# Weight pairs' high and low parts in new homes, the third pair made in the first FFN pass, rows of sums issued every second product

## The chip, the cores and the metric

The kernel runs on one core of one Trainium2 chip. The metric is the device time of one execution in microseconds, lower is better. TensorE (PE) multiplies, VectorE (DVE) and ScalarE (ACT) do the arithmetic around it, GpSimd (POOL) helps in the first half, and SyncE (SP) issues nearly all transfers (DMAs).

## The reference

Attention in which a query sees only the keys of its own hash bucket, and then a feed-forward layer (FFN) over all 3072 tokens. Inputs and output are float32.

```python
q, k, v: (4, 8, 768, 64); proj: (64, 6); w_in: (512, 2048); w_out: (2048, 512)
bucket = sum(2**n * (x @ proj > 0)[n])            # for q and for k
scores = where(q_bucket == k_bucket, q @ k.T / 8, -1e9)
attn   = exp(scores - max);  attn = attn / (attn.sum() + 1e-9)
x      = (attn @ v) of the heads side by side      # (3072, 512)
h      = x @ w_in
g      = h if h >= 1, 0 if h <= -1, (h + 1)**2 / 4 between
out    = g @ w_out
```

## The kernel before

Float32 accuracy comes from splitting each operand into a high part, rounded to the type float32r, and the rest, the low part: a product is then three matmuls, high x high, low x high, high x low.

The first half, to about 470 us, is attention, head after head. It leaves x unnormalised in DRAM, along with the sums to divide by, and prepares most weights on the way. This text is about the second half, `ffn`, which has two stages.

In the **first pass** the two chunks of 384 tokens of batch 0 go through the FFN in 32 steps (`gemm1`, L795 to L805, one f tile of 128 hidden features a step; N1 = 32). In the **second stage** the three other batches are computed with seven products in place of eight (a Strassen-Winograd scheme over two token chunks and two f tiles): L882 to L932 run 168 products, 7 for each of 8 pairs of f tiles for each of 3 batches. Here product k is number k from the first pass's end; the code writes it N1 + k. A product is six matmuls of 384 columns (L898), and between products four to six matmuls of 512 columns of the second layer are issued from a queue (`issue`, L674). The seven results combine in two PSUM banks and three SBUF tiles: after product s of a pair VectorE or ScalarE reads the bank (L902 to L918; s = 1 is L905), and products 2, 3 and 6 add onto a bank that was read before.

The seven products need seven blocks of weights for each pair, kept in DRAM (`wc`): blocks 0 to 2 are copies (`w_plain`), blocks 3 to 6 are sums and differences, made on the chip once, while the first batch's products already run. A pair's four sums are made so: `w_get` (the fetch, L740, L741) brings raw weights into `tmp`; `w_sum` in three parts makes the four sums in `sum_w` on VectorE (its subtractions have line 39, that of the helper `sub`); `w_hi` rounds them on ScalarE into `hi_w`, the other half of `tmp`; `w_lo` subtracts in place, so that the low parts replace the sums in `sum_w`; `w_put` (the put, L756, L757) sends both parts, 512 KB each, to `wc`. `w_plan` says in which step each of this happens. `sum_w` has one buffer: the next pair's first sum can only start when the put of the low parts has landed. Before, pairs 0 and 1 are made in the first pass, pair 2 by product 5, and pair i from there at 7 (i - 2): its fetch is in product 7 (i - 2) - 3, its sums in + 1 and + 2, its put in + 5.

The products' weights come back through a ring of nine slots (`w_load`, L775, 256 KB each), each issued eight products ahead.

The x operands of a batch (`x_plan`) need x in pieces (`x_raw`, L691, into `pcs`), rows of sums spread over the partitions (`x_er`, two transfers of 192 KB a step, L537, into a place that `spread` names and that is not in use yet, the home of an operand that is made later), normalisation on VectorE (`x_norm`, L698 and L700), sums (L709), high and low parts. Two sets of homes (`sets`: pieces of `big`, `ta`, `tb`, `tu`, `tmp`, all tiles of earlier use) serve the batches in turn.

The order of the instructions on each engine is written out by hand: `at` puts a function ahead of a step's or product's matmuls, `after` behind them, and each engine works through its own list in order, held up by the semaphores of what it needs. SyncE too is one list: a transfer that has to wait holds up all behind it.

Of the kernel before, what the change touches and what calls it, by code (L numbers as in the profile page):

```python
# [11 lines left out]
F32 = mybir.dt.float32  # L12
# [562 lines left out]
def ffn(ctx, tc, wpair, woh, wol, xm, xa, xb, areas, wst, wq, wc, out, prep, post, staged):  # L575
# [35 lines left out]
    def spread(b, cc, k):  # L611

        if b > 1:
            x = sets[(b - 1) % 2]
            n = (14, 16, 18, 25)[k]
            t, n = (tb, 6) if x is sets[1] and n == 14 else (big, n + 12) if x is sets[1] and n < 20 else (
                tu, 0) if x is sets[1] else (big, n)
        else:
            t, n = (ta, 2 * k) if cc == 1 else (tflat, 2 * k) if k < 2 else (sflat, 0) if k == 2 else (
                pcs.rearrange("p k n -> p (k n)"), 4)  # L620
        return t[:, n * CH:(n + 2) * CH].bitcast(F32).rearrange("p (t n) -> p t n", t=2)
# [126 lines left out]
    def w_hi(n):  # L748
        nc.scalar.copy(out=hi_w[:, 2 * n:2 * n + 2], in_=sum_w[:, 2 * n:2 * n + 2])

    def w_lo(n):
        sl = slice(2 * n, 2 * n + 2)
        sub(nc, nc.vector, sum_w[:, sl].bitcast(F32R), sum_w[:, sl], hi_w[:, sl].bitcast(F32))

    def w_put(i):
        nc.sync.dma_start(out=wc[i][:, 3:7, 0], in_=hi_w.bitcast(F32))  # L756
        nc.sync.dma_start(out=wc[i][:, 3:7, 1], in_=sum_w)  # L757

    def w_plan(i, get, first, second, his, los, put):
        at(get, w_get, i)  # L760
        at(first, w_sum, 0)
        at(second, w_sum, 1)
        at(second, w_sum, 2)
        for t in range(2):
            after(his[t], w_hi, t)
            at(los[t], w_lo, t)
        at(put, w_put, i)
# [48 lines left out]
    w_plan(0, 21, 24, 25, (25, 25), (26, 26), 27)  # L816
    w_plan(1, 26, 28, 29, (29, 29), (30, 30), 31)
    w_plan(2, 30, N1 + 1, N1 + 2, (N1 + 2, N1 + 3), (N1 + 4, N1 + 4), N1 + 5)
    for i in range(3, NFT // 2):
        n = N1 + NBLK * (i - 2)  # L820
        w_plan(i, n - 3, n + 1, n + 2, (n + 2, n + 3), (n + 4, n + 4), n + 5)
    x_plan(1, 0, 8, (8, 9, 10, 11), (11, 12, 13, 14), range(15, 22))
    x_plan(1, 1, 22, (24, 24, 25, 25), (26, 26, 27, 27), (28, 28, 29, 29, 30, 30, 31))
    x_plan(2, 0, N1 + 6, range(N1 + 6, N1 + 10), [N1 + n for n in (13, 14, 17, 20)],
           [N1 + n for n in (21, 24, 27, 28, 31, 34, 35)])
    x_plan(2, 1, N1 + 37, [N1 + n for n in (28, 30, 32, 34)], [N1 + n for n in (41, 42, 44, 46)],
# [10 lines left out]
    at(30, ring_staged)  # L837
# [290 lines left out]
```

## Time and profile before

| | us |
|---|---|
| median of 3 runs | 1004.57 (1003.85, 1004.57, 1008.62) |
| profiled execution | 1005.65, its span 1003.9 |
| busy in the span: PE, DVE, ACT, POOL | 972.9, 794.0, 680.7, 344.3 |
| first product of the second stage starts | 600.87 |

Times in the rows are microseconds from the start of the span. A timeline row has the start, the duration, the engine, the line and the operation, what it writes and reads (buffer numbers are left out: `t` stands for several tiles, among them a slot of the ring), and in brackets how long the engine was idle before it and what ended that. A row with x6 is six instructions merged. Line 898 is a product's matmuls. The number of a product can be counted from 600.87; one takes about 2.2 us, so product 10 starts at 622.77. Durations of matmuls overlap, so the steps between their starts count. Engines that wait for a transfer wait for its landing, of which a row of the chain of waits gives the time: a row that begins with DMA runs from issue to landing.

### The profile page before, as it was taken

What the parts mean: (1) busy time and instruction counts of PE and PEld (TensorE: products, weight loads), DVE (VectorE), ACT (ScalarE), POOL (GpSimd) and SP (SyncE); (2) the same over time, 40 slices, a digit from 0 to 9 for tenths busy, and PEclk for the clock granted to TensorE, in tenths of its full rate; (3) what the DMA queues carried; (4) which work ended last, traced back from release to release, by engine and by line L of the source; (5) the groups of instructions that cost most, each with busy time, mean ns of one, the idle gap of its engine ahead of it and who ended that gap; (6) DMA issues with size and microseconds to landing.
All of it is one profiled execution on the core that took longest, in us unless ns stands there. A gap on an engine that the chain in (4) does not pass through costs nothing.

```text
span 1003.9 us, 15529 instructions
## 1 busy us (share of the span) xinstructions
PE 972.9 (97%) x5036; PEld 891.9 (89%) x5036; DVE 794.0 (79%) x1356; ACT 680.7 (68%) x1489; POOL 344.3 (34%) x412
## 2 busy tenths in 40 slices
PE   5899999999999999999999999799999999999997
PEld 4789999999999999999999998688888898888896
DVE  7678999999999999886998687678766677655553
ACT  5778889988999888888655465355554455554443
POOL 6666778778877777656000000000000000000000
PEclk9999999999999999999999999899999999999999
DMA  2646667666666666645494358878549564454431
GB/s 90 164 113 150 174 186 196 188 179 161 173 161 171 175 174 184 156 111 131 141 329 138 116 196 262 253 225 262 149 141 247 146 185 117 134 163 116 117 84 64
DMA packets 94170, 166.19 MB, mean 166 GB/s; under 512 B 13833, under 2 KB 51337, under 8 KB 94089
## 3 DMA queue, kind: packets, MB, share of 16 engines
q1 hardware_dynamic: 93872, 165.19, 58.5%
q8 instruction: 40, 0.66, 0.3%
q14 instruction: 42, 0.34, 0.1%
q10 hardware_dynamic: 216, 0.00, 0.0%
HBM read 106.13 MB, written 33.87 MB: 139 GB/s over the span
## 4 chain that ended last, share of the span: by engine, by line
PE 84%; DVE 6%; ACT 4%; DMA 3%; issue 1%; SPq 0%; POOL 0%; ACTq 0%; DVEq 0%
PE y L674 23%; PE h L898 15%; PE smax L258 7%; PE h L802 7%; PE o L332 6%; PE s L298 6%; PE o L330 6%; PE o L331 6%; PE s L297 6%; DMA t<-ed 2%; PE o L178 2%; DVE nm L262 2%; DMA wc<-sumw 1%; ACT t L633 1%; DVE nm L359 1%
## 5 line engine op out<-in xcount | busy, mean ns | idle before, releaser
L306 ACT ACTIVATE ph<-s 128x384 fp32r<-128x384 f32 x380 | 188.4, 496 | 45.1 <-PE s L298 38.0
L262 DVE TENSOR_REDUCE nm<-smax 128x1 f32<-128x768 f32 x186 | 176.2, 947 | 16.3 <-PE smax L258 14.5
L39 POOL TENSOR_TENSOR pl<-pf,ph 128x384 fp32r<-128x384 f32 x128 | 141.7, 1112 | 79.1 <-ACT pf L311 78.6
L639 DVE SCALAR_TENSOR_TENSOR t<-t 128x384 f32<-128x384 f32 x128 | 71.3, 557 | 115.4 <-ACT z L634 115.2
L39 DVE TENSOR_TENSOR pl<-s,ph 128x384 fp32r<-128x384 f32 x256 | 135.7, 545 | 14.8 <-ACT s L311 14.1
L297 PE MATMUL s<-t 128*128 128x384 f32 x384 | 132.0, 344 | 0.8 <-DVE t L212 0.8
L332 PE MATMUL o<-pl,va 128*128 128x386 f32 x384 | 130.3, 339 | 0.3 <-DVE pl L39 0.3
L330 PE MATMUL o<-ph,va 128*128 128x386 f32 x384 | 130.2, 339 | 0.0
L298 PE MATMUL s<-t 128*128 128x384 f32 x384 | 130.1, 339 | 0.0
L331 PE MATMUL o<-ph,vb 128*128 128x386 f32 x384 | 129.4, 337 | 0.0
L311 ACT ACTIVATE s<-s 128x384 f32<-128x384 f32 x252 | 125.5, 498 | 0.0
L674 PE MATMUL y<-t,ghi 128*128 128x512 f32 x384 | 125.5, 398 | 0.0
L258 PE MATMUL smax<-t 128*128 128x384 f32 x372 | 101.5, 353 | 5.6 <-DVE nm L262 4.5
L898 PE MATMUL h<-wbig,t 128*128 128x384 f32 x399 | 83.0, 341 | 5.4 <-DVE wsq L905 5.4
L644 ACT CAST ghi<-z 128x384 fp32r<-128x384 f32 x129 | 65.1, 505 | 29.1 <-DVE z L640 25.8
L633 ACT ACTIVATE t<-h,mh 128x384 f32<-128x384 f32 x56 | 32.5, 581 | 77.1 <-PE h L802 48.3
L258 PEld LDWEIGHTS smax<-t 128*128 128x128 f32 x372 | 63.7, 188 | 22.5 <-DVE nm L262 21.3
L898 PEld LDWEIGHTS h<-wbig,t 128*128 128x128 f32 x399 | 71.9, 190 | 12.6 <-DVE wsq L905 6.7
L633 ACT ACTIVATE t<-wsq,mh 128x384 f32<-128x384 f32 x48 | 29.6, 617 | 77.5 <-DVE wsq L911 44.6
L674 PEld LDWEIGHTS y<-t,ghi 128*128 128x128 f32 x384 | 71.9, 189 | 11.2 <-ACT ghi L644 0.3
L634 ACT ACTIVATE z<-t,m 128x384 f32<-128x384 f32 x128 | 79.0, 617 | 4.2
L674 PE MATMUL y<-woh,ghi 128*128 128x512 f32 x192 | 75.6, 394 | 0.7 <-ACT ghi L644 0.7
(153 smaller groups left out, 2143.8 us busy)
## 6 DMA issues: line engine op xcount, KB each, us to landing
t<-wc SPq DMA_DIRECT2D x92, 256.0 KB
t<-t SPq DMA_DIRECT2D x60, 384.0 KB
wraw<-wc SPq DMA_DIRECT2D x76, 256.0 KB
raw<-in_qk_dram SPq DMA_DIRECT2D x15, 768.0 KB
wraw<-in_w_in_dram SPq DMA_DIRECT2D x16, 512.0 KB
wraw<-in_w_out_dram SPq DMA_DIRECT2D x16, 512.0 KB
xd<-xs SPq DMA_DIRECT2D x32, 192.5 KB
vraw<-in_v_dram SPq DMA_DIRECT2D x16, 384.0 KB
```

The lines of the kernel that those rows point to most:

```text
L39: eng.tensor_tensor(out=out, in0=a, in1=b, op=ALU.subtract)
L258: nc.tensor.matmul(out=smax[hd][:, hf, 0:HS], lhsT=t2[:, 0, h, i * P:(i + 1) * P], rhs=t2[:, 1, h, hf * HS:(hf + 1) * HS], start=True, sto ...
L262: nc.vector.tensor_reduce(out=nmp(hd)[:, i:i + 1], in_=smax[hd][:, :, 0:HS], axis=AX.XY, op=ALU.max, negate=True)
L297: nc.tensor.matmul(out=ps[:, 0:HS], lhsT=t1[:, 1, h, ks], rhs=t1[:, 0, h, sl], start=True, stop=False)
L298: nc.tensor.matmul(out=ps[:, 0:HS], lhsT=t2[:, 1, h, ks], rhs=t2[:, 0, h, sl], start=False, stop=True)
L306: nc.scalar.activation(out=ph[:, 0:HS], in_=ps[:, 0:HS], func=AF.Exp, scale=SCALE)
L311: nc.scalar.activation(out=pf, in_=ps[:, 0:HS], func=AF.Exp, scale=SCALE)
L330: nc.tensor.matmul(out=o, lhsT=wa, rhs=ph, start=(jj == 0), stop=False)
L331: nc.tensor.matmul(out=o, lhsT=wb, rhs=ph, start=False, stop=False)
L332: nc.tensor.matmul(out=o, lhsT=wa, rhs=pl, start=False, stop=(jj == NJ - 1))
L674: nc.tensor.matmul(out=ys[c][m], lhsT=g_[:, m * P:(m + 1) * P], rhs=w, start=(first and k == 0), stop=(last and k == 2))
L898: nc.tensor.matmul(out=ps, lhsT=w[:, cs], rhs=x, start=(n == 0 and s not in (2, 3, 6)), stop=(n == 5), skip_group_check=True)
```

## The change

There are three parts. **Homes of the parts:** from pair 3 on the low parts are written to the end of `big` and no longer over the sums, and the high parts of odd pairs go to `tu`, those of even pairs stay in `hi_w`. These places are homes of x operands that are made later. **Pairs earlier:** pairs 0 to 2 are made in the first pass, at steps 19 + 4 i to 24 + 4 i, and pair i from 3 on at 7 (i - 3): fetch at - 2, sums at + 1 and + 2, put at + 5, so that at product 12 the put of pair 4 and then the fetch of pair 5 are issued. **Rows of sums:** those of batch 2 are issued in products 7, 9, 11 and 13 for the first half (before: 6, 7, 8, 9) and 34 to 37 for the second, into other places, since `big` and `tu` are in use; normalisation of the first half is in 15, 17, 20, 21 (before: 13, 14, 17, 20). Batch 3's rows of sums get other places too. The ring's first loads are issued two steps earlier.

```diff
@@ -610,11 +610,10 @@
 
     def spread(b, cc, k):
 
-        if b > 1:
-            x = sets[(b - 1) % 2]
-            n = (14, 16, 18, 25)[k]
-            t, n = (tb, 6) if x is sets[1] and n == 14 else (big, n + 12) if x is sets[1] and n < 20 else (
-                tu, 0) if x is sets[1] else (big, n)
+        if b == 2:
+            t, n = (ta, 2 * k) if cc == 0 else ((tb, 6), (big, 28), (big, 30), (tu, 0))[k]
+        elif b == 3:
+            t, n = big, 2 * NBLK * cc + 2 * k
         else:
             t, n = (ta, 2 * k) if cc == 1 else (tflat, 2 * k) if k < 2 else (sflat, 0) if k == 2 else (
                 pcs.rearrange("p k n -> p (k n)"), 4)
@@ -745,16 +744,25 @@
         o, x, y = ((t[:, 0:2], r[:, 1:3], r[:, 0:2]), (t[:, 2], r[:, 2], t[:, 0]), (t[:, 3], t[:, 2], r[:, 3]))[part]
         sub(nc, nc.vector, o, x, y)
 
-    def w_hi(n):
-        nc.scalar.copy(out=hi_w[:, 2 * n:2 * n + 2], in_=sum_w[:, 2 * n:2 * n + 2])
-
-    def w_lo(n):
+    def w_homes(i):
+
+        def four(t, n):
+            return t[:, n:n + 4 * HM].rearrange("p (b n) -> p b n", b=4)
+        return (hi_w if i < 3 or i % 2 == 0 else four(tu, 0),
+                sum_w.bitcast(F32R) if i < 3 else four(big, 28 * CH))
+
+    def w_hi(i, n):
         sl = slice(2 * n, 2 * n + 2)
-        sub(nc, nc.vector, sum_w[:, sl].bitcast(F32R), sum_w[:, sl], hi_w[:, sl].bitcast(F32))
+        nc.scalar.copy(out=w_homes(i)[0][:, sl], in_=sum_w[:, sl])
+
+    def w_lo(i, n):
+        sl = slice(2 * n, 2 * n + 2)
+        hi, lo = w_homes(i)
+        sub(nc, nc.vector, lo[:, sl], sum_w[:, sl], hi[:, sl].bitcast(F32))
 
     def w_put(i):
-        nc.sync.dma_start(out=wc[i][:, 3:7, 0], in_=hi_w.bitcast(F32))
-        nc.sync.dma_start(out=wc[i][:, 3:7, 1], in_=sum_w)
+        for t, w in enumerate(w_homes(i)):
+            nc.sync.dma_start(out=wc[i][:, 3:7, t], in_=w.bitcast(F32))
 
     def w_plan(i, get, first, second, his, los, put):
         at(get, w_get, i)
@@ -762,8 +770,8 @@
         at(second, w_sum, 1)
         at(second, w_sum, 2)
         for t in range(2):
-            after(his[t], w_hi, t)
-            at(los[t], w_lo, t)
+            after(his[t], w_hi, i, t)
+            at(los[t], w_lo, i, t)
         at(put, w_put, i)
 
     ring = [tu[:, n * DM:(n + 1) * DM] for n in range(3, 6)] + [wpair[15][:, t] for t in range(2)]
@@ -813,17 +821,17 @@
                 (xm.make, (1, ct, part, *xs[1], [nc.vector] * 2)))
     for i in range(NFT // 2):
         at(8 + i, w_plain, i)
-    w_plan(0, 21, 24, 25, (25, 25), (26, 26), 27)
-    w_plan(1, 26, 28, 29, (29, 29), (30, 30), 31)
-    w_plan(2, 30, N1 + 1, N1 + 2, (N1 + 2, N1 + 3), (N1 + 4, N1 + 4), N1 + 5)
+    for i in range(3):
+        n = 19 + 4 * i
+        w_plan(i, n, n + 2, n + 3, (n + 3, n + 3), (n + 4, n + 4), n + 5)
     for i in range(3, NFT // 2):
-        n = N1 + NBLK * (i - 2)
-        w_plan(i, n - 3, n + 1, n + 2, (n + 2, n + 3), (n + 4, n + 4), n + 5)
+        n = N1 + NBLK * (i - 3)
+        w_plan(i, n - 2, n + 1, n + 2, (n + 2, n + 3), (n + 4, n + 4), n + 5)
     x_plan(1, 0, 8, (8, 9, 10, 11), (11, 12, 13, 14), range(15, 22))
     x_plan(1, 1, 22, (24, 24, 25, 25), (26, 26, 27, 27), (28, 28, 29, 29, 30, 30, 31))
-    x_plan(2, 0, N1 + 6, range(N1 + 6, N1 + 10), [N1 + n for n in (13, 14, 17, 20)],
-           [N1 + n for n in (21, 24, 27, 28, 31, 34, 35)])
-    x_plan(2, 1, N1 + 37, [N1 + n for n in (28, 30, 32, 34)], [N1 + n for n in (41, 42, 44, 46)],
+    x_plan(2, 0, N1 + 7, range(N1 + 7, N1 + 15, 2), [N1 + n for n in (15, 17, 20, 21)],
+           [N1 + n for n in (23, 24, 27, 28, 31, 34, 35)])
+    x_plan(2, 1, N1 + 37, range(N1 + 34, N1 + 38), [N1 + n for n in (41, 42, 44, 46)],
            range(N1 + 47, N1 + 54))
     N3 = N1 + 56
     x_plan(3, 0, N3 + 8, range(N3 + 8, N3 + 12), [N3 + n for n in (15, 16, 18, 22)],
@@ -834,7 +842,7 @@
     at(N1 + 5, xm.sums_add)
     at(N1 + 5, xm.sums_inv, B - 1)
 
-    at(30, ring_staged)
+    at(28, ring_staged)
     for k in range(4, NRING):
         at(N1 + (k > 6), w_load, k)
 
```

How the lists of SyncE and VectorE change is shown at three places. Names: `wc_97` to `wc_104` are the DRAM tensors of pairs 0 to 7, `wq_81` to `wq_96` the raw weights (two for a pair), `ed_69` the sums and `xd_61` the x of batch 2, `ed_70` and `out_dram` belong to batch 3 and to the output, `xsva` holds a column of x. `wraw`, `t_1_75` and `t_2_76` as the target of a load are ring slots; `t_1_75` is also `tu`, `wbig` also `big`, `t_1_78` is `ta`, `t_2_79` is `tb`.

SyncE before, from the load in product 5 to the raw x of batch 2 in product 6:

```order
L775 DMA t_1_75<-wc_98 128x512
L756 DMA wc_99<-tmp 128x4x256
L757 DMA wc_99<-sumw 128x4x256
L527 DMA ed_70<-pcs 8x16x48
L664 DMA out_dram<-ot 128x512 x2
L775 DMA t_1_75<-wc_99 128x512
L689 DMA xsva<-xd_61 128x4x2
L691 DMA pcs<-xd_61 128x2x384 x2
```

SyncE now, from the same load to the raw x, now in product 7:

```order
L783 DMA t_1_75<-wc_98 128x512
L765 DMA wc_100<-t_1_75 128x4x256
L765 DMA wc_100<-wbig 128x4x256
L739 DMA tmp<-wq_89 128x2x256
L740 DMA tmp<-wq_90 128x512
L527 DMA ed_70<-pcs 8x16x48
L663 DMA out_dram<-ot 128x512 x2
L783 DMA t_1_75<-wc_99 128x512 x2
L688 DMA xsva<-xd_61 128x4x2
L690 DMA pcs<-xd_61 128x2x384 x2
```

Pair 3's put stands where pair 2's stood, the fetch of pair 4 follows it, and two loads of the ring now come before the raw x.

SyncE before, in products 7 to 12, behind a first pair of rows of sums (into `t_2_79`, product 6):

```order
L775 DMA t_1_75<-wc_99 128x512
L537 DMA wbig<-ed_69 64x2x384 x2
L775 DMA t_2_76<-wc_99 128x512
L537 DMA wbig<-ed_69 64x2x384 x2
L775 DMA t_2_76<-wc_99 128x512
L537 DMA t_1_75<-ed_69 64x2x384 x2
L775 DMA wraw<-wc_99 128x512 x2
L740 DMA tmp<-wq_89 128x2x256
L741 DMA tmp<-wq_90 128x512
L775 DMA wraw<-wc_99 128x512
L756 DMA wc_100<-tmp 128x4x256
L757 DMA wc_100<-sumw 128x4x256
```

SyncE now, in products 7 to 13, from the first pair of rows of sums:

```order
L537 DMA t_1_78<-ed_69 64x2x384 x2
L783 DMA t_2_76<-wc_99 128x512 x2
L537 DMA t_1_78<-ed_69 64x2x384 x2
L783 DMA wraw<-wc_99 128x512 x2
L537 DMA t_1_78<-ed_69 64x2x384 x2
L783 DMA wraw<-wc_99 128x512
L765 DMA wc_101<-tmp 128x4x256
L765 DMA wc_101<-wbig 128x4x256
L739 DMA tmp<-wq_91 128x2x256
L740 DMA tmp<-wq_92 128x512
L783 DMA wraw<-wc_100 128x512
L537 DMA t_1_78<-ed_69 64x2x384 x2
```

Rows of sums alternate with two loads in place of one, their last pair has moved behind the put, the put is that of pair 4 in place of pair 3, and a fetch follows it where one stood ahead of it.

VectorE before, products 13 to 15, around the first sum of pair 4 (`sumw<-tmp`):

```order
L698 SCALAR_TENSOR_TENSOR pcs<-t_2_79,xsva,pcs 128x384
L700 TENSOR_TENSOR pcs<-pcs,t_2_79 128x384
L917 TENSOR_TENSOR wsq<-h_6046,wsq 128x384
L648 TENSOR_TENSOR glo<-z,ghi 128x384
L639 SCALAR_TENSOR_TENSOR t<-t 128x384
L640 TENSOR_TENSOR z<-t,z 128x384
L698 SCALAR_TENSOR_TENSOR pcs<-wbig,xsva,pcs 128x384
L700 TENSOR_TENSOR pcs<-pcs,wbig 128x384
L648 TENSOR_TENSOR glo<-z,ghi 128x384
L39 TENSOR_TENSOR sumw<-tmp 128x512
L905 TENSOR_TENSOR wsq<-h_6046,wsq 128x384
L648 TENSOR_TENSOR glo<-z,ghi 128x384
```

VectorE now, products 13 to 15, around the first sum of pair 5 (line 913 is what line 905 was, 697 and 699 are 698 and 700):

```order
L925 TENSOR_TENSOR wsq<-h_6046,wsq 128x384
L647 TENSOR_TENSOR glo<-z,ghi 128x384
L638 SCALAR_TENSOR_TENSOR t<-t 128x384
L639 TENSOR_TENSOR z<-t,z 128x384
L647 TENSOR_TENSOR glo<-z,ghi 128x384
L39 TENSOR_TENSOR sumw<-tmp 128x512
L697 SCALAR_TENSOR_TENSOR pcs<-t_1_78,xsva,pcs 128x384
L699 TENSOR_TENSOR pcs<-pcs,t_1_78 128x384
L913 TENSOR_TENSOR wsq<-h_6046,wsq 128x384
L647 TENSOR_TENSOR glo<-z,ghi 128x384
L39 TENSOR_TENSOR sumw<-tmp,sumw 128x256
```

The first two steps of normalisation are gone from products 13 and 14; the first one stands between the sum and the read of the bank in product 15.

## Rows read from the trace of the kernel before

**Rows 1.** the page: busy time, share of the span, instructions of each engine

```profile
PE 972.9 (97%) x5036; PEld 891.9 (89%) x5036; DVE 794.0 (79%) x1356; ACT 680.7 (68%) x1489; POOL 344.3 (34%) x412
```

**Rows 2.** waits of TensorE after 500 us: us in total, times, longest

```profile
PE h L898 <- DVE wsq L905: 5.8, 2, 5.4
```

**Rows 3.** timeline of TensorE: start, us, instruction [idle before, releaser]

```profile
622.77 1.22 PE L898 MATMUL h<-wbig,wraw 128*128 128x384 f32 x6
...
644.08 2.29 PE L898 MATMUL h<-wbig,t 128*128 128x384 f32 x6 [5.37 <-DVE wsq L905]
...
650.98 1.22 PE L898 MATMUL h<-wbig,wraw 128*128 128x384 f32 x6
...
655.66 1.21 PE L898 MATMUL h<-wbig,wraw 128*128 128x384 f32 x6
...
657.88 1.21 PE L898 MATMUL h<-wbig,t 128*128 128x384 f32 x6
```

**Rows 4.** windows: length, busy of PE, PEld, DVE, ACT, POOL; clock, DMA, GB/s

```profile
550.00:560.00 10.00, 10.00 (x52) 9.06 (x51) 8.59 (x18) 5.31 (x11) 0.00 (x0) 1.00 0.00 0
600.00:620.00 20.00, 20.00 (x100) 17.79 (x99) 13.57 (x29) 11.34 (x23) 0.00 (x0) 1.00 0.83 275
620.00:640.00 20.00, 18.71 (x93) 16.35 (x91) 14.34 (x28) 9.91 (x19) 0.00 (x0) 1.00 1.06 272
638.71:644.08 5.37, 0.01 (x1) 0.00 (x0) 1.21 (x3) 0.59 (x2) 0.00 (x0) 0.85 0.64 220
644.08:650.98 6.90, 6.90 (x22) 6.20 (x23) 5.92 (x12) 1.63 (x4) 0.00 (x0) 0.62 0.81 263
650.98:657.88 6.90, 6.90 (x36) 6.16 (x35) 4.59 (x10) 2.74 (x6) 0.00 (x0) 1.00 0.72 232
```

**Rows 5.** timeline of TensorE around 696 us

```profile
695.60 1.31 PE L898 MATMUL h<-wbig,wraw 128*128 128x384 f32 x6 [0.46 <-DVE wsq L905]
```

**Rows 6.** timeline of VectorE, products 8 to 17

```profile
620.85 0.68 DVE L39 TENSOR_TENSOR sumw<-tmp 128x512 f32<-128x512 f32 x1
...
632.16 0.61 DVE L698 SCALAR_TENSOR_TENSOR pcs<-t,xsva,pcs 128x384 f32<-128x384 f32 x1
...
633.29 0.55 DVE L917 TENSOR_TENSOR wsq<-h,wsq 128x384 f32<-128x384 f32 x1
...
642.87 0.69 DVE L39 TENSOR_TENSOR sumw<-tmp 128x512 f32<-128x512 f32 x1 [4.95 <-DMA wc<-sumw]
```

**Rows 7.** chain of waits from 600 to 650: start, us, what

```profile
621.34 6.65 DMA t<-ed
...
628.01 8.32 DMA t<-ed
...
636.39 6.45 DMA wc<-sumw
```

**Rows 8.** timeline of SyncE's queue, its issues

```profile
564.43 5.17 SPq L537 DMA_DIRECT2D t<-ed  x8
...
613.53 0.38 SPq L775 DMA_DIRECT2D t<-wc  x1
...
615.05 1.03 SPq L527 DMA_DIRECT2D ed<-pcs  x1
```

**Rows 9.** DMA issues after 500 us: transfer, queue, count, KB each

```profile
t<-wc SPq DMA_DIRECT2D x92, 256.0 KB
...
tmp<-wq SPq DMA_DIRECT2D x16, 256.0 KB
wc<-tmp SPq DMA_DIRECT2D x8, 512.0 KB
...
t<-ed SPq DMA_DIRECT2D x16, 192.0 KB
```

**Rows 10.** timeline of VectorE in the first pass

```profile
566.74 0.56 DVE L639 SCALAR_TENSOR_TENSOR t<-t 128x384 f32<-128x384 f32 x1 [2.56 <-ACT z L634]
...
577.87 0.61 DVE L698 SCALAR_TENSOR_TENSOR pcs<-t,xsvb,pcs 128x384 f32<-128x384 f32 x1
```

## The prediction

> **What bounds the kernel now.** I read the page's busy shares first, then the waits of TensorE in the second half, then the instructions around the one long wait, and last the chain of waits through it.
>
> TensorE is busy 97% of the span [rows 1]. From 500 us on it waits little: the list of what it waited for has one large entry, 5.8 us for VectorE's line 905 in two waits, the longest 5.4 [rows 2]. So at most one place is worth much, and I price that place. TensorE starts product 17 at 644.08 after 5.37 us of idleness [rows 3]. The granted clock is 1.00 later on but 0.62 on average in the 6.90 us from that restart, so partly at 1.2 GHz, and 22 matmuls start there where the next 6.90 us have 36 [rows 4]. In products: 17 and 18 take the 6.90 us from 644.08 to 650.98, where one takes 2.22 afterwards (655.66 to 657.88) [rows 3]; 6.90 - 2 x 2.22 = 2.46 us lost to the clock. The place costs 5.37 + 2.46 = 7.8 us, 0.8% of the time. No edit to this stage can win much more; the other idle moments are like the 0.46 us at 696 [rows 5].
>
> Why it stops: product 17 adds onto a bank that VectorE must first have read (line 905, of product 15). VectorE stands 4.95 us before the first sum of pair 4, which overwrites sumw, until the transfer of pair 3's low part out of sumw has landed [rows 6]; then come the sum, line 905, TensorE. The chain goes back from there through three transfers, each from issue to landing: rows of sums, issued at 621.34, landed 6.65 us on at 627.99; others issued at 628.01 landed at 636.33; the put issued at 636.39 landed at 642.84 [rows 7]. In SyncE's order (third order rows in the section on the change, which begin right after the first of these) the second is the eighth transfer after the first, and the put the eighth after that. So SyncE runs eight transfers ahead of the landings, which come in the order of issue here, and the put landed late because the 16 transfers before it were slow, not for its own 512 KB. The DMA engines' share from 620 to 640 is 1.06 [rows 4]: the queue is full there.
>
> **The change part by part.** (1) Low parts go to a home of their own, so from pair 3 on no sum waits for a put of low parts. The 4.95 us wait as it stands is gone. (2) But pair 5 now stands where pair 4 stood: its first sum, still in product 15, needs its raw weights. Before, pair 4's were fetched at product 11, ahead of the put; now pair 5's are fetched at product 12, and stand on SyncE behind both halves of pair 4's put (fourth order rows). What is late next is the landing of that fetch, behind the same full queue. This decides my forecast, so I work out when it lands.
>
> Let L be 256 KB of weights (a load, or half a fetch), 2L half a put (512 KB), and e one transfer of rows of sums (192 KB) [rows 9]. Between the landings at 627.99 and 636.33 three loads and five e landed: 3L + 5e = 8.34. Between 636.33 and 642.84 it was one e, three loads, two halves of a fetch and two of a put: 9L + e = 6.51. That gives L = 0.58 and e = 1.32 us, an estimate from [rows 7]. From SyncE's load at 613.53 [rows 8] to the transfer that VectorE waits for (first to fourth order rows), before has 8 loads, 8 e, 2 halves of a fetch, 4 of a put, and sundries. After has, to the second half of pair 5's fetch, 8 loads, 6 e (two have moved behind), 4 halves of a fetch, 4 of a put, and the same sundries. The difference is 2L - 2e = -1.5 us: the fetch lands at about 642.84 - 1.5 = 641.3. Bounds: with e by its bytes alone (0.75 L, so L = 0.67) it is +0.3; with e at its largest (8.34 / 5 = 1.67, loads free there; L = 0.54) -2.3. So 640.5 to 643.1; I take the solution of the two equations.
>
> Behind the waiting sum VectorE now has two instructions of normalisation ahead of the read that TensorE needs, since x_norm's first step moves from product 13 to 15 (fifth and sixth order rows). The pair takes 633.29 - 632.16 = 1.13 us [rows 6]. Before, the restart came 644.08 - 642.84 = 1.24 us after the landing. So TensorE restarts at 641.3 + 1.24 + 1.13 = 643.7 instead of 644.08: 0.4 us gained; by the bounds between 642.9 (1.2 gained) and 645.5 (1.4 lost). The idle stretch stays near 5 us, so I leave the clock's 2.5 us as they are.
>
> (3) The third pair moves into the first pass, and pair 0 to steps 21 to 23. VectorE gets some 2.9 us more there (three sums and two low parts, 0.4 to 0.7 us each by [rows 6]). It is busy 8.59 of 10 us from 550 [rows 4], but stands 2.56 us idle in a later step [rows 10], and TensorE waits for none of it: cost nothing, 2.9 at most without that cover. Pair 0's put and pair 1's fetch go ahead of eight rows of sums on SyncE (4L + 2L = 3.5 us later); those were issued from 564.43 for 5.17 us [rows 8] and are first read at 577.87 [rows 10]: nothing, up to 1 us if they are late. In this pass sums still wait for puts; the list of TensorE's waits has no such wait from before 600 as its cause.
>
> (4) Rows of sums issued every second product spread eight transfers over seven products. Ahead of product 15's fetch that takes away only the two e that I counted. (5) The second set of rows of sums, now at products 34 to 37, goes to places which the last put (product 33) frees. SyncE may stand a few us; the loads behind it are issued eight products (18 us) ahead: nothing, 1 us at most. (6) The last pair is done at product 33 instead of 40, so VectorE is freer where TensorE lost 0.46 us at 696, but x_norm's last step and a pair's first sum now meet in products 21 and 22. I set one against the other: 0, from -0.7 to +0.7. (7) The last batch's new places of rows of sums: addresses only, 0.
>
> Sum: -0.4 us. The profiled execution took 1005.65 us (1.75 around its span), so 1005.3 by it; the median of the runs is 1.08 below that execution, and I forecast 1004.57 - 0.4 = 1004.2 us. The likeliest case's own range is -1.2 - 0.7 to +1.4 + 0.7 about the median: 1002.7 to 1006.7.
>
> **Rivals.** A. The wait goes. For that the fetch must land before 638.71 (where the idle stretch begins) - 1.24 - 1.13 = 636.3, five us before my estimate. For it: the change frees sumw, which the profile names as what VectorE waited for. Against it: that put was the last of a full queue, and the fetch takes its place there. Price: all 7.8 us, 996.8.
>
> B. It goes by half: the fetch lands 2 to 3 us earlier than I think, TensorE idles some 2.5 us, and the clock has not fallen by then (0.85 on average over the 5.37 idle us [rows 4], so it fell towards their end). Then 0.4 + 2.5 + 2.46 = 5.4 us gained: 999.2. For it: e is uncertain, and two equations are a thin base. Against it: my lower bound is 640.5. The Trainium skill's page "DMA: Bandwidth & Descriptors", section "Queues, rings and completion order", says that completion is not in order per issuing engine. By that rule the fetch could land ahead of the put it stands behind, 4L earlier at 639.0, which is this rival; the three landings in the trace's chain each let the eighth next issue go, in order, and I give the rule little.
>
> C. Slower. From pair 3 on, the fetch stands right behind a put, so pair 4's first sum, in product 8, could wait too. VectorE reached that sum at 620.85 [rows 6]; with 1.24 us from there to the restart, and product 10 starting at 622.77 [rows 3], there is 0.7 us of room. Pair 4's fetch will be issued about where SyncE had 615.05 [rows 8]. If it takes the 8.32 us that rows of sums took in a full queue, it lands at 623.9 and TensorE stands 2.4 us; with the upper bound at product 15 (+1.4) that is 1008.4. It decides from a landing at 621.5 on. Against it: the DMA share is 0.83 from 600 to 620 [rows 4], so the queue is not full there, and only some 7L = 4 us of transfers stand from 613.53 on.
>
> D. The change doesn't do what it says: the one home of the low parts makes each of them wait for the put before it. That put is issued six products earlier and ahead of the fetch in the queue, so it lands first: no.
>
> **How the numbers follow.** Likeliest case 0.73, A 0.08, B 0.09, C 0.07, D and what I don't see 0.03. About 0.5%, 5.0 us, is what a measurement of this kernel can tell from no change. Faster by more: A, and most of B: 0.17 with a little of the unseen. Slower by more needs C and something beside it: 0.06. Same: 0.77. The range leaves out A, part of B, and C's tail: 999.8 to 1007.2.
>
> **What would show it.** In the new profile TensorE still has one idle stretch of 4 to 7 us, ahead of product 17, near 643, with the clock down behind it. VectorE's wait there is no longer for the put out of sumw but for the fetch (tmp from wq), ends near 641, and is followed by sum, normalisation and the read. If the stretch is under 3 us or gone, my count of the queue was wrong; if the wait is for something else, the mechanism was; if product 10 waits, C is right.

## The result and the profile after

The changed kernel takes 1008.34 us (median of 22 runs, 1005.48 to 1011.47) where the kernel before takes 1005.48 beside it: a ratio of 1.0028, 95% interval 1.0018 to 1.0037. The forecast was 1004.2 with a range to 1007.2. The difference stays within 0.5%, as the likeliest case had it, but its sign is the other one and the time lies 1.1 us beyond the range. Of that, 0.9 us is the base: the forecast was counted from three runs (1004.57), and counted from 1005.48 its upper bound would be 1008.1. The profiled execution took 1008.66 us.

TensorE is as busy as in [rows 1], and again one wait stands out; it is for the same read of VectorE, in the changed kernel at line 913 [rows 2]. The page's line of busy times, changed kernel:

```profile
PE 975.6 (97%) x5036; PEld 895.0 (89%) x5036; DVE 794.3 (79%) x1356; ACT 680.8 (68%) x1489; POOL 344.2 (34%) x412
```

Its waits of TensorE after 500 us:

```profile
PE h L906 <- DVE wsq L913: 7.2, 2, 6.9
PE h L906 <- DVE wsq L925: 0.7, 3, 0.3
```

The timeline of TensorE around it, to be held against [rows 3]. Product 0 starts at 602.75, 1.88 us later than before; product 17 is the row with the wait, and product 19 starts at 653.98:

```profile
602.75 1.22 PE L906 MATMUL h<-wbig,wraw 128*128 128x384 f32 x6
...
647.46 2.29 PE L906 MATMUL h<-wbig,t 128*128 128x384 f32 x6 [6.87 <-DVE wsq L913]
...
653.98 1.22 PE L906 MATMUL h<-wbig,wraw 128*128 128x384 f32 x6
656.20 1.22 PE L906 MATMUL h<-wbig,wraw 128*128 128x384 f32 x6
```

The idle stretch is 1.50 us longer than the 5.37 of [rows 3]. Products 17 and 18 take 6.52 us together, where the product after them takes 2.22: 2.08 us go to the clock, where it was 2.46. The granted clock in the windows (length, PE busy, clock, DMA share, GB/s; the idle stretch, 6.90 us from the restart, and after it), the answer to [rows 4]:

```profile
640.59:647.46 6.87, 0.01 (x2) 0.82 0.99 306
647.46:654.36 6.90, 6.90 (x25) 0.68 0.23 53
654.36:660.00 5.64, 5.64 (x30) 1.00 1.02 342
```

So the place costs 8.95 us instead of 7.83: 1.12 more. From product 0 to the end the two traces differ by just that (404.1 and 403.0 us). The other 1.88 us of their spans lie ahead of the FFN's first pass, in code that the change doesn't touch: that pass starts at 474.83 instead of 472.96, and takes 127.92 us in the one and 127.91 in the other.

What VectorE did meanwhile, the answer to [rows 6]; its first row is the first sum of product 8, its second that of product 15:

```profile
623.25 0.69 DVE L39 TENSOR_TENSOR sumw<-tmp 128x512 f32<-128x512 f32 x1 [0.44 <-DMA tmp<-wq]
...
645.12 0.69 DVE L39 TENSOR_TENSOR sumw<-tmp 128x512 f32<-128x512 f32 x1 [7.39 <-DMA tmp<-wq]
645.73 0.61 DVE L697 SCALAR_TENSOR_TENSOR pcs<-t,xsva,pcs 128x384 f32<-128x384 f32 x1
646.38 0.56 DVE L699 TENSOR_TENSOR pcs<-pcs,t 128x384 f32<-128x384 f32 x1
646.85 0.55 DVE L913 TENSOR_TENSOR wsq<-h,wsq 128x384 f32<-128x384 f32 x1
```

The wait is for the fetch now, no longer for the put, and behind the sum come two instructions of normalisation and then the read. The chain of waits, beside [rows 7], ends the same way:

```profile
629.80 7.78 DMA wraw<-wc
...
637.60 7.43 DMA tmp<-wq
```

The fetch landed at 645.03, which is 42.3 us after product 0. The forecast of 641.3 is 40.4 us after product 0 of the kernel before, its bounds 39.6 to 42.2. The restart came 2.43 us behind the landing (forecast 1.24 + 1.13 = 2.37).

### The profile page after: what moved, and what is told of

The parts are those of the page before. It is cut to its first block, busy times and chain, and to the rows that moved or that the text cites. A ratio compares the mean times of both kernels' runs of the same rounds, so it can differ in the third digit from the quotient of the medians.

```text
span 1006.9 us, 15529 instructions
## 1 busy us (share of the span) xinstructions
PE 975.6 (97%) x5036; PEld 895.0 (89%) x5036; DVE 794.3 (79%) x1356; ACT 680.8 (68%) x1489; POOL 344.2 (34%) x412
## 4 chain that ended last, share of the span: by engine, by line
PE 83%; DVE 8%; ACT 4%; DMA 3%; issue 1%; POOL 0%; SPq 0%; ACTq 0%; DVEq 0%
PE y L673 21%; PE h L906 14%; PE smax L258 7%; PE h L810 7%; PE o L332 6%; PE s L298 6%; PE o L330 6%; PE o L331 6%; PE s L297 6%; PE o L178 2%; DVE nm L262 2%; DVE t L638 1%; ACT z L633 1%; ACT t L632 1%; DVE z L639 1%
## 5 line engine op out<-in xcount | busy, mean ns | idle before, releaser
L632 ACT ACTIVATE t<-wsq,mh 128x384 f32<-128x384 f32 x48 | 29.6, 617 | 76.5 <-DVE wsq L919 44.7
```

## The experiments

One table serves all of them. "Landing" is when the transfer landed that the first sum of product 15 waited for, in us after product 0 of that trace; "halves" is how long each half of the fetch took to land behind the transfer before it; both are worked out from the issue and landing times in the traces. "Idle" is TensorE's longest wait between products 16 and 19, in the profiled run. Ratios are to runs of the kernel before on the same chip, with the 95% interval. A trace is of one execution: those of h and f are the fastest of their kernel (1002.97 and 998.50 us), those of c and e the slowest (1008.48 and 1010.25), so a landing and a median need not belong together.

```
kernel             landing        halves     idle  ratio (interval)
before             42.0 (put)     .70 .66    5.37  1
before, again      42.6 (put)     .70 .66    5.95  0.9999 (0.9982-1.0016)
the change         42.3 (fetch)  1.23 1.21   6.87  1.0028 (1.0018-1.0037)
a fetch ahead      36.0 (fetch)  1.49 .77    0.56  0.9956 (0.9943-0.9969)
b norm at 16       41.4 (fetch)  1.03 1.04   4.74  1.0019 (1.0010-1.0027)
c rows at 17       41.4 (fetch)   .75 .68    5.93  1.0018 (1.0008-1.0027)
d homes alone      37.7 (fetch)   .70 .67    1.16  0.9957 (0.9945-0.9969)
e order alone      43.1 (fetch)  1.22 1.39   7.69  1.0024 (1.0014-1.0034)
f no rows          34.3 (fetch)   .72 .68    0     0.9943 (0.9928-0.9959)
h put late         38.9 (fetch)   .75 .96    3.53  1.0001 (0.9990-1.0012)
g sums moved too   36.5 (fetch)  1.36 1.08   0     0.9952 (0.9939-0.9966)
i sum at 16        43.5 (fetch)  1.24 1.16   5.65  1.0001 (0.9990-1.0013)
j norms moved      36.3 (fetch)  1.17 .61    0     0.9942 (0.9927-0.9958)
k fetch at 10      34.2 (fetch)   .82 1.16   0     0.9936 (0.9921-0.9950)
```

The change, b, e and i have the same transfers in the same order ahead of that landing and behind it, and still their landings lie between 41.4 and 43.5: a single trace sizes this term to about a microsecond.

**a. The fetch ahead of the put.**

```diff
-        w_plan(i, n - 2, n + 1, n + 2, ...)
+        w_plan(i, n - 3 + (i == 3), n + 1, n + 2, ...)
```

> The changed kernel with one thing altered: pairs 4, 5 and 6 are fetched one product earlier (pair 5 at product 11), so that pair 5's fetch stands on SyncE ahead of pair 4's put instead of behind it; pair 3 is fetched as before. My account (VectorE's first sum of product 15 waits for a fetch that stands in a full queue; what is ahead of it sets its landing): the fetch is freed of the two halves of a put, 512 KB each, ahead of it, so it lands 2.5 to 4 us earlier than the 645.0 of the changed kernel's trace; TensorE's idle time before product 17 goes from 6.87 us to 3 or 4 us, or less, and the time falls by 3 to 5 us against the changed kernel (1003 to 1005 us), and by up to 2.5 us more if the clock no longer falls. Rival (the fetch is slow of itself wherever it stands, since the transfers that follow it share the engines): it lands no more than 1 us earlier, and the time falls by at most 1 us.

Median 1000.65. Timelines of VectorE and TensorE at the place:

```profile
637.20 0.69 DVE L39 TENSOR_TENSOR sumw<-tmp 128x512 f32<-128x512 f32 x1 [1.27 <-DMA tmp<-wq]
...
639.53 1.31 PE L906 MATMUL h<-wbig,t 128*128 128x384 f32 x6 [0.56 <-DVE wsq L913]
...
652.14 1.31 PE L906 MATMUL h<-wbig,t 128*128 128x384 f32 x6 [1.00 <-DVE wsq L925]
```

The wait goes nearly whole, the granted clock stays 1.00 in the 6.90 us from the restart, and the median is 7.7 us below the changed kernel's. The landing moved by 6.3 us, more than I expected: besides the put, the fetch also passed a pair of rows of sums and a load, which I had not counted. The rival falls. So the place of the fetch in the queue decides. (The edit moves pair 7's fetch too, here and in g, j and k; that comes later than the place read here.)

**b. The normalisation behind the read.**

```diff
-    ... [N1 + n for n in (15, 17, 20, 21)],
+    ... [N1 + n for n in (16, 17, 20, 21)],
```

> The changed kernel with one thing altered: the first step of the normalisation for batch 2's first half stands at product 16 instead of 15, behind the read that TensorE waits for instead of ahead of it. My account (after the landing come in turn the sum, two instructions of normalisation and the read; all on the path): the fetch lands as before, the read comes 1.1 us earlier, TensorE's idle time before product 17 goes from 6.9 to about 5.8 us, the time falls by 1.1 us to about 1007.2. Rival (the read waits for something else as well, or the landing moves): no change in the idle time, 0 us.

1007.18. VectorE and TensorE:

```profile
645.15 0.69 DVE L39 TENSOR_TENSOR sumw<-tmp 128x512 f32<-128x512 f32 x1 [6.29 <-DMA tmp<-wq]
645.76 0.55 DVE L913 TENSOR_TENSOR wsq<-h,wsq 128x384 f32<-128x384 f32 x1
...
646.37 2.29 PE L906 MATMUL h<-wbig,t 128*128 128x384 f32 x6 [4.74 <-DVE wsq L913]
```

From landing (645.06) to restart it is 1.31 us instead of 2.43: the 1.12 us are shown. The idle time fell by 2.13, but the other 1.0 is mostly the earlier landing of this trace (0.90). In the time the 1.1 us can't be told: the interval overlaps that of the change.

**c. The rows of sums behind the fetch issued later.**

```diff
-    x_plan(2, 0, N1 + 7, range(N1 + 7, N1 + 15, 2), ...
+    x_plan(2, 0, N1 + 7, [N1 + n for n in (7, 9, 11, 17)], ...
```

> The changed kernel with one thing altered: the last two transfers of rows of sums of batch 2's first half, which SyncE issues right behind pair 5's fetch at product 13, are issued at product 17 instead. Nothing ahead of the fetch changes. Theory of the transfers behind (SyncE issues ahead of the landings, so that transfers issued behind the fetch run beside it on the same engines and slow its packets, 1.2 us for each half where I had estimated 0.58): the fetch lands about 1.2 us earlier, TensorE's idle time before product 17 is 5.5 to 6 us, the time falls by about 1.2 us. Theory of the put ahead (the engines that lag with the put's packets make the fetch late): the fetch lands within 0.3 us of where it did, and the time stays within 0.5 us.

1006.72. TensorE:

```profile
646.76 2.29 PE L906 MATMUL h<-wbig,t 128*128 128x384 f32 x6 [5.93 <-DVE wsq L913]
```

The halves fell from 1.23 and 1.21 to 0.75 and 0.68, with the put still ahead of them. The landing came 0.9 us before that of the changed kernel's trace and 1.2 before the mean of the four alike (42.6), so alone it would not settle it, since b landed as early without this edit. The halves do, for pair 5's fetch: wherever no rows of sums are issued in the 3 us behind the fetch (both traces of before, c, d, f) they take 1.36 to 1.43 us together; wherever some are (the change, a, b, e, g to k) 1.71 to 2.61.

**d. The homes alone.**

```diff
+    lo_big = big[:, 28 * CH:28 * CH + 4 * HM].rearrange("p (b n) -> p b n", b=4)
+    def w_home(i):
+        return lo_big if 3 <= i <= 6 else sum_w.bitcast(F32R)
...
-        sub(nc, nc.vector, sum_w[:, sl].bitcast(F32R), ...)
+        sub(nc, nc.vector, w_home(i)[:, sl], ...)
...
-        if b > 1:
+        if b == 2 and cc == 0:
+            t, n = ta, 2 * k
+        elif b > 1:
```

> The kernel before with one thing of the change taken over: from pair 3 on low parts go to a home of their own (the last places of big), and the rows of sums of batch 2's first half that stood there go to ta. The order of all steps is that of the kernel before, with pair 4's fetch at product 11 ahead of pair 3's put. My account: VectorE's first sum of product 15 now waits for the fetch alone, which landed at 639.55 in the trace of before, where the put out of sumw landed at 642.84; so TensorE restarts 3.3 us earlier, idles about 2 us instead of 5.4, and the clock probably does not fall any more: 3.3 to 5.8 us less than before, about 999 to 1001. Rival (the wait is put down to the put in the trace, but it is the queue that is late, and with the put's wait gone something else ends it at the same time): within 1 us of before.

1000.71. VectorE, then TensorE:

```profile
639.60 0.69 DVE L39 TENSOR_TENSOR sumw<-tmp 128x512 f32<-128x512 f32 x1 [0.77 <-DMA tmp<-wq]
...
640.82 1.31 PE L905 MATMUL h<-wbig,t 128*128 128x384 f32 x6 [1.16 <-DVE wsq L912]
...
653.43 1.31 PE L905 MATMUL h<-wbig,t 128*128 128x384 f32 x6 [1.00 <-DVE wsq L924]
```

(Pair 7's low parts stay in sumw here; no pair comes after it.) The edit of the change that frees sumw is worth 4.6 us by itself, as long as the fetch stays ahead of the put. The clock didn't fall (granted 1.00 in the 6.90 us from 640.82). About 1.5 us come back in small waits further on, of which 1.00 is the last row.

**e. The order alone.**

```diff
-        return (hi_w if i < 3 or i % 2 == 0 else four(tu, 0),
-                sum_w.bitcast(F32R) if i < 3 else four(big, 28 * CH))
+        return hi_w, sum_w.bitcast(F32R)
```

> The changed kernel without the new homes: high and low parts stay where they were (hi_w and sumw) for all pairs; the order of pairs, fetches and rows of sums is that of the change. My account (in the change's order the last thing to land for the first sum of product 15 is pair 5's fetch, which stands on SyncE behind both halves of pair 4's put, so the put out of sumw lands about 2.4 us before it, and the homes win nothing in this order): TensorE's idle time before product 17 stays at 6 to 7 us, the wait there is again put down to the fetch, and the time is that of the changed kernel, 1008 us, within 1.5. Rival (without homes some other sum or high part waits for a put as well, in product 8 or 22): a second idle stretch and 1010 us or more.

1007.36, and the wait is the fetch's:

```profile
646.00 0.69 DVE L39 TENSOR_TENSOR sumw<-tmp 128x512 f32<-128x512 f32 x1 [8.20 <-DMA tmp<-wq]
...
648.34 2.29 PE L905 MATMUL h<-wbig,t 128*128 128x384 f32 x6 [7.69 <-DVE wsq L912]
```

In this order the homes win nothing: the put out of sumw landed at 643.27, 2.61 us before the fetch. There is no second long idle stretch, so the rival falls. With d, this splits the change: homes -4.6 us in the old order, 0 in the new one; the new order is what loses.

**f. Without the rows of sums.**

```diff
-            at(er[k], x_er, b, cc, k)
+            if (b, cc) != (2, 0):
+                at(er[k], x_er, b, cc, k)
```

> The changed kernel without the eight transfers of rows of sums for batch 2's first half (that half is then normalised with what lay in their places). Six of them stood ahead of pair 5's fetch. By the size in my prediction (1.32 us of queue each) the fetch lands 7.9 us earlier, 33.5 to 34.5 us after product 0 starts, where it was 42.3 in the changed kernel's trace and 41.4 in two others; no idle time before product 17, no fall of the clock there, and 999 us or less. By their bytes alone (0.5 us each) it lands 3.0 us earlier, 38.5 to 39.5 after product 0, TensorE still idles about 4 us, and the time is about 1005.

999.72, 0.7 us more than the 999 I named, and in the timeline of TensorE no idle moment from product 0 to product 21:

```profile
650.58 1.31 PE L907 MATMUL h<-wbig,t 128*128 128x384 f32 x6 [0.46 <-DVE wsq L926]
655.73 1.31 PE L907 MATMUL h<-wbig,t 128*128 128x384 f32 x6 [0.46 <-DVE wsq L914]
```

The fetch landed 8.0 us earlier; 1.04 of that are its own halves (1.40 instead of 2.44), so the six transfers ahead cost 7.0, or 1.16 each; 1.2 by the mean of the four landings. My 1.32 was near, their bytes (0.5) are not: next to weights a transfer of rows of sums takes more than twice its share.

**h. The put behind the fetch.**

```diff
-        at(put, w_put, i)
+        at(put + 2 * (i == 4), w_put, i)
```

> The changed kernel with one thing altered: pair 4's put (two transfers of 512 KB) is issued at product 14 instead of 12, behind pair 5's fetch instead of ahead of it; nothing is left out. By what the halves of the put took at the end of the queue in all traces (1.3 us each) the fetch lands 2.6 us earlier; TensorE's idle time before product 17 is about 4 us (6.9 less 2.6), the time about 1005.5 us. Rival (what is issued behind the fetch slows it about as much as what is ahead, since the queue's transfers share the engines): the fetch lands less than 1.3 us earlier and the idle time is over 5.5 us, about 1007. Theory that a put ahead slows the fetch's own halves: these take 0.7 us each instead of 1.0 to 1.2; theory that rows of sums behind it do: they stay at 1.0 to 1.2.

1005.49. Timelines of VectorE and TensorE:

```profile
639.98 0.69 DVE L39 TENSOR_TENSOR sumw<-tmp 128x512 f32<-128x512 f32 x1 [4.25 <-DMA tmp<-wq]
...
642.31 1.63 PE L906 MATMUL h<-wbig,t 128*128 128x384 f32 x6 [3.53 <-DVE wsq L913]
...
648.40 1.22 PE L906 MATMUL h<-wbig,wraw 128*128 128x384 f32 x6
```

The landing moved by 3.3 us (expected 2.6), and by 2.4 against the earliest of the four traces with the change's order; the idle time is 3.53. This trace is of the fastest execution, but the median too lies where it was expected: the put ahead is worth about its full time, and the rival falls. The halves took 0.75 and 0.96, between the two theories' figures: the rows of sums were issued somewhat further behind here.

**g. Everything off the read.**

```diff
-        w_plan(i, n - 2, n + 1, n + 2, ...)
+        w_plan(i, n - 3 + (i == 3), n + 2, n + 2, ...)
...
-    ... (15, 17, 20, 21)], ... (23, 24, 27, 28, 31, 34, 35)
+    ... (16, 18, 19, 21)], ... (23, 24, 25, 28, 31, 32, 35)
```

> A version meant to beat both: the changed kernel with pairs 4 to 6 fetched a product earlier, all three sums of a pair from pair 3 on one product later (behind the read that TensorE waits for, instead of the first one ahead of it), the normalisation's steps at products 16, 18, 19 and 21, none of which has such a read, and two later steps of that half moved off products 27 and 34. The version with the earlier fetch alone kept five idle moments of TensorE, 0.56, 1.00, 0.45, 0.18 and 0.21 us, each with VectorE's read behind a sum or a step of normalisation. My account: these go, no new one comes, 2.4 us less than that version's 1000.65: about 998.3. Rival (VectorE's load is the bound there, and the work that moves delays another read by as much): within 0.7 us of 1000.65.

1000.54: the rival. (Of a pair's three sums the edit moves only the first; the other two stood there already.) The two longest of its idle moments:

```profile
650.93 1.33 PE L906 MATMUL h<-wbig,wraw 128*128 128x384 f32 x6 [0.94 <-DVE wa L922]
...
668.42 1.31 PE L906 MATMUL h<-wbig,wraw 128*128 128x384 f32 x6 [0.61 <-DVE wa L922]
```

The waits changed their read (line 922 instead of 913), and in sum they grew, from 2.40 us in a to 3.08 up to product 40.

**i. The first sum a product later.**

```diff
-        w_plan(i, n - 2, n + 1, n + 2, ...)
+        w_plan(i, n - 2, n + 2, n + 2, ...)
```

> The changed kernel with one thing altered: from pair 3 on the first sum of a pair stands one product later, so that VectorE meets the wait for pair 5's fetch at product 16, behind the read of product 15 instead of ahead of it. My account: product 17 starts without a wait; the fetch lands as before, 41.4 to 43.1 us after product 0 starts; behind it VectorE has three sums, a step of normalisation and an activation's end (about 4 us) ahead of the read of product 17, which product 19 needs: TensorE idles 3.5 to 5 us there instead of 6.9 ahead of product 17, and the time is about 1006. Rival (the wait is as long wherever it stands, since all that VectorE has to do comes behind it): 6 us or more ahead of product 19, and 1008.

1005.82, and the wait moves to product 19:

```profile
646.01 0.69 DVE L39 TENSOR_TENSOR sumw<-tmp 128x512 f32<-128x512 f32 x1 [6.77 <-DMA tmp<-wq]
...
649.72 0.55 DVE L917 TENSOR_TENSOR wa<-h,wsq 128x384 f32<-128x384 f32 x1
...
650.32 2.29 PE L906 MATMUL h<-wbig,wraw 128*128 128x384 f32 x6 [5.65 <-DVE wa L917]
```

As expected in place and time; the idle time of 5.65 is over the 5 that I had as its upper end and under the rival's 6, in a trace whose fetch landed late (43.5, expected 43.1 at most). The time decides for my account. From the sum to the restart it is now 4.3 us, but TensorE has two products more to do meanwhile.

**j and k. The normalisation in products without a read, the fetch earlier still.** j is a with this edit; k has the second line in place of a's:

```diff
-    ... [N1 + n for n in (15, 17, 20, 21)],
+    ... [N1 + n for n in (14, 16, 18, 23)],
...
+        w_plan(i, n - 4 + 2 * (i == 3), n + 1, n + 2, ...)
```

> The version with pairs 4 to 6 fetched a product earlier, and the normalisation's steps at products 14, 16, 18 and 23 instead of 15, 17, 20 and 21. That version's two largest idle moments (0.56 us ahead of product 17, 1.00 us ahead of product 22) each had a step of normalisation ahead of VectorE's read. My account: both go, 1.0 to 1.5 us less than its 1000.65: about 999.3. Rival (as in the version with sums moved too, the work that moves delays another read as much): 1000 to 1001.

> As the version with the steps of normalisation at products 14, 16, 18 and 23, with pairs 4 to 6 fetched one product earlier still (pair 5 at product 10, ahead of the second pair of rows of sums). My account: the fetch lands another 2.0 to 2.6 us earlier (two rows of sums fewer ahead of it), but VectorE hardly waited for it any more: the same time within 0.5 us. Rival (rows of sums that now land later are waited for by a step of normalisation at product 14 or 16): an idle moment of 1 to 2 us ahead of product 16 or 17, and 1 to 2 us more.

1000.14 and 999.25. What is left of TensorE's waits between products 17 and 32, j and then k:

```profile
649.07 1.31 PE L906 MATMUL h<-wbig,wraw 128*128 128x384 f32 x6 [0.24 <-DVE wa L922]
652.02 1.33 PE L906 MATMUL h<-wbig,t 128*128 128x384 f32 x6 [0.48 <-DVE wsq L925]
668.94 1.32 PE L906 MATMUL h<-wbig,wraw 128*128 128x384 f32 x6 [0.88 <-DVE wsq L925]
```

```profile
651.50 1.34 PE L906 MATMUL h<-wbig,t 128*128 128x384 f32 x6 [0.46 <-DVE wsq L925]
668.42 1.31 PE L906 MATMUL h<-wbig,wraw 128*128 128x384 f32 x6 [0.89 <-DVE wsq L925]
```

a's 0.56 is gone and its 1.00 is halved, but a new 0.88 stands at 668.94, so j wins less than expected and cannot be told from a. k's fetch landed 2.1 us before j's, as expected, and k takes 999.25, 0.9 below j where I had allowed 0.5; their intervals overlap. It has the lowest median here: 0.64% faster than the kernel before (0.50 to 0.79%), 9 us faster than the changed one.

**The kernel before, a second time.**

> The kernel before, unaltered, for a second trace of it: the landing that a stall hangs on differs from execution to execution. In its first trace the put out of sumw landed 42.0 us after product 0 starts; with only the homes added, the same queue landed it at 41.0; in four traces with the changed order of transfers the fetch that VectorE waits for landed at 41.4 to 43.5, mean 42.6. If the change made that landing later on the mean (my account: the fetch's halves, slowed by the rows of sums behind them, eat up what the two rows moved behind gave), this trace lands the put at 41 to 42 with TensorE idle 4.3 to 5.5 us ahead of product 17. Rival (the first trace of before was an early one, and both orders land alike): 42.5 or later and 6 us or more.

```profile
643.74 0.69 DVE L39 TENSOR_TENSOR sumw<-tmp 128x512 f32<-128x512 f32 x1 [5.54 <-DMA wc<-sumw]
...
644.96 2.29 PE L898 MATMUL h<-wbig,t 128*128 128x384 f32 x6 [5.95 <-DVE wsq L905]
```

The put landed at 42.6, the rival's side of the line, with the idle time just under its 6. So that the landing itself is later on the mean in the new order isn't shown: 42.3 over the two traces of before, 42.6 over the four of the new order, with a scatter of 1 us. That it didn't come 1.5 us earlier, as forecast, is.

## Why the prediction was right and wrong

**The mechanism held, step by step.** One idle stretch stays, ahead of product 17, with the clock down behind it. VectorE's wait is for the fetch instead of the put (the change's trace; e), and it is the fetch's place behind the put that makes it late (a, h). The 1.13 us of normalisation come on top (1.12 in b). Rival A's price holds only in part: with the fetch moved up, the long wait and the clock's loss go, but a's time is 4.6 us under that of the kernel before, not 7.8. In a's trace the stretch from product 0 to the end is 5.7 us shorter than before's (397.3 against 403.0), and new idle moments (0.56 and 1.00 us the longest) take some of the rest.

**What failed is the landing of the fetch**, in the step "The difference is 2L - 2e = -1.5 us: the fetch lands at about 642.84 - 1.5 = 641.3." The price e is near (f: about 1.2, I had 1.32). L is not: I priced half a fetch at 0.58 wherever it stands, from two stretches of the queue. In the trace of before a half took 0.68; in the changed kernel 1.22. Pair 5's two halves cost 2.44 instead of 1.16, and c shows most of why, with d and f beside it: with the two rows of sums that the change moved behind the fetch out of the way, they cost 1.43. The sentence "Ahead of product 15's fetch that takes away only the two e that I counted" took what is issued behind as free; it gave back about 1 us of the 2.6 that moving them had won. Pair 4's fetch, also counted at 0.58 a half, took 1.21 and 0.66. Together the four halves cost 4.31 in the change, where before's two cost 1.36: 2.95 more instead of 2L = 1.16. These 1.8 us are the miss (42.3 forecast as 40.4, all after product 0).

That sum closes more neatly than it deserves, since a landing varies by a microsecond from trace to trace and the other terms are right only together. Between the same two landings the sundries, counted as equal, took 6.9 us instead of 4.8; the seven loads, counted as equal, 6.1 instead of 8.6; the rows of sums 3.7 (six) instead of 6.1 (eight). So a single landing's step isn't the price of that transfer, and what is shown is what single edits give: about 1 us of the 1.8 is the rows of sums behind the fetch (c), and 0.3, an estimate, is e (1.16 by f for 1.32, twice). The remaining 0.5 stays open. Pair 4's slow first half in particular is not from rows of sums behind it: it took 1.04 in f, which has none, and 0.88 to 1.49 in b, c, e, h and i.

**The restart** then lies at 42.3 + 2.4 = 44.7 us after product 0 instead of 43.2: 1.5 us lost where 0.4 were to be gained. The clock gives back 0.4. In this trace the landing lies at my upper bound, by which I had priced 1.4 us of loss; three traces of the same order lie on either side of it, so the bounds were too narrow for one landing, too.

**The rest of the difference** is not settled. The stall explains 1.1 us between the two profiled executions and 1.2 by the idle times of like traces (6.87 and 7.69 against 5.37 and 5.95, mean 1.6, less the clock's 0.4). The change's 22 runs are 2.9 us slower. e, with the same order and a like stall, is 1.9 us slower than the kernel before beside it, and there the mean granted clock of whole runs is alike (0.9957 and 0.9958). The stretch ahead of the first pass differs from 472.96 to 475.76 us over all traces, in code that is the same in each, so a single pair of profiles can't show a shift of a microsecond there. Part of the 1.88 us between the two traces is the clock, near the start. Windows of the first 40 us, before and then changed (length, PE busy, clock, DMA share, GB/s):

```profile
0.00:40.00 40.00, 24.98 (x113) 1.00 0.43 121
0.00:40.00 40.00, 26.12 (x102) 0.91 0.41 119
```

b and g show the 0.91 too; c, e and i reach the first pass late (474.5 to 475.1) without it. Over whole runs the mean granted clock was 0.9946 for the change's 22, and 0.9948 to 0.9963 for the kernel before in the four sets run beside the experiments. So that the change makes the clock fall more often isn't shown.

**What was priced at nothing** cost nothing. The third pair in the first pass: that pass takes 127.9 us in every trace, before and after. The other idle moments sum to 1.06 us (0.33, 0.18, 0.23, 0.32) where they were 1.01 (0.21, 0.46, 0.34). Rival C's place shows: VectorE stood 0.44 us at product 8's sum for pair 4's fetch, but TensorE didn't wait. Rival B's rule of the Trainium skill ("DMA: Bandwidth & Descriptors", "Queues, rings and completion order"), that completion is not in order per issuing engine, did not show for the fetch: it landed behind the put it was issued behind, at 645.03 after 642.59, in this trace and in b, c, e, f and i. The section's own example is a later transfer on fewer engines than the one ahead of it, and that did show: `ed<-pcs` (8 partitions; 9 updates of its semaphore where the put has 16) landed at 619.34 in the trace of before, ahead of the put issued before it (619.40). Rival B's step from the rule to a fetch that passes the put, both with 16 updates, went further than that example.

## What to carry to other kernels

When an edit removes a wait, look up what is issued last in the same queue and will be waited for next; here freeing a buffer was worth 4.6 us by itself, and with the reordering that came with it the kernel was 2.9 us slower than before. A transfer waited for soon belongs ahead of large writes that nobody waits for. Price a transfer in a full queue by its neighbours on both sides, not by its bytes or by its place in the row alone, and take several traces where the whole forecast hangs on one landing.

## What the runs showed of the hardware

Packets of weights were slower beside rows of sums, and not beside a put. In the traces' packet records, over the stretch in which pair 5's fetch landed, packets of 2048 bytes took 84 and 86 ns on the mean in c and f, where none of 1536 bytes (rows of sums) ran beside them; in the changed kernel, beside 159 of those (115 ns), they took 128 ns, in e and i 157 and 155, in h and k 98 and 116. In before, over the landing of pair 4's fetch, they took 87 ns beside 428 packets of 1024 bytes, the put's.

The clock did not fall after every wait: the granted clock stayed 1.00 over the 6.90 us behind idle times of 0.56 us (a) and 1.16 (d), and was 0.75 there on the mean behind 3.53 (h), where it had still been 1.00 during the wait itself. Windows of a, d and then h (length, PE busy, clock, DMA share, GB/s):

```profile
639.53:646.43 6.90, 6.90 (x34) 1.00 1.05 340
640.82:647.72 6.90, 6.90 (x34) 1.00 0.62 201
638.78:642.31 3.53, 0.00 (x1) 1.00 1.08 248
642.31:649.21 6.90, 6.90 (x27) 0.75 0.88 304
649.21:655.00 5.79, 5.79 (x30) 1.00 1.04 350
```

So the fall can come after the restart. Products 17 and 18 took 6.09 us in h (642.31 to 648.40), 1.65 more than twice 2.22; behind before's 5.37 us of idleness that loss was 2.46.
